# Attention's softmax in a fused attention and expert kernel: the maximum subtracted on VectorE, one exponential per half unit in a stage of its own

## The chip, the cores and the metric

One core of one Trainium2 chip runs the whole program. The metric is the device time of one execution in microseconds, as the median of several runs. The engines named below are TensorE (matrix products and transposes), VectorE, ScalarE, GpSimd and SyncE (whose queue, SP, issues nearly all transfers). Each engine takes its instructions in a fixed order, written at build time.

## What is computed

Three parts in a row, in fp32. First a chunked attention over 2 batches, 8 heads, 768 positions of 64 values, with 8 memory keys ahead of every chunk's own context. Then a layer of 4 experts, weighted by normalized probabilities. Then a two-matrix layer whose activation has a slope of its own for negative values.

```python
for c in range(nc):                       # chunks of 32; 16 keys to the left, 8 to the right
    scores = scale * np.matmul(q_c, k_full.transpose(0, 1, 3, 2))
    scores = scores - np.max(scores, axis=-1, keepdims=True)
    a = np.exp(scores)
    a = a / (np.sum(a, axis=-1, keepdims=True) + 1e-09)
    out[:, :, c_start:c_end] = np.matmul(a, v_full)
...
for e in range(E):
    h = np.maximum(x @ w1[e], 0.0)
    out += p[:, e:e + 1] * (h @ w2[e])
...
h = x @ w_in
g = np.maximum(h, 0.0) + alpha * np.minimum(h, 0.0)
return (g @ w_out).astype(np.float32)
```

## The kernel before

**Attention** is cut into 16 units of 96 queries (3 chunks, told apart by a mask that rides in extra rows of the operands) and each into two half units of 4 heads, 32 in all. `half_unit` (lines 191 to 246) is a generator; each `yield` ends a stage and gives the planner the lag until the next one. Its stages are these. (1) Four products `s` into one PSUM bank, 96x512; VectorE's maximum `mx` of each head; `nm`, the maximum times minus the scale, on VectorE; four exponentials on ScalarE, one per head, each with its `nm` as bias, from PSUM into `pe`. (2) Four transposes `t` of `pe` on TensorE, copied by ScalarE into `pt_ring`. (3) Four products `x` of `pt_ring` and the values, whose extra column of ones gives the denominator; `dn`, `rd` and the scaling into `xs_ring` on VectorE. (4) Two transposes `xt`, copied by ScalarE into `acc`; after a pair of units, `prep_x` makes the differences and the high and low parts of the next layer's input, on VectorE for the first two column blocks and on GpSimd for the others. `pe`, `pt_ring` and `xs_ring` have two slots each, by half unit; `qk` has three (`RING`) and `v` four (`RINGV`), and each is loaded again as soon as the stage that reads it has been written down.

**The planner.** There is no scheduler behind the kernel: `keep_in_program_order` holds each engine to the order in which the code calls it, and the code calls it along a planned clock `now`, which only TensorE's instructions move. `att_poll` (line 250) goes on with the first half unit whose lag is over, at most `LIVE` at a time, and starts a new one every `PACE`. Where nothing is due and it is forced, `fill` writes matmuls on a tile of zeros (`warm`) for the planned idle time. The lags are `LAT`, in planned us after each stage.

**Around it.** Names after the attention: `a`, `b`, `c`, `d` are the products of an expert's first matrix (`gemm1`, a fast scheme with seven products in place of eight), `y` those of the second (`gemm2`), each in a high and low split; `g` and `gg` are the activations, `wh` and `wl` the high and low part of the weights, made by a stream `prep_w` on ScalarE and VectorE (the first two pairs) or GpSimd. The columns go in two halves of 384. Attention is forced until 16 half units are done, enough for the first half; then come `gemm1` of the first pair for the first half (no attention in it, `hold`), `gemm2` with attention between its products, the forced rest of attention, and the same pair for the second half. From there on the work is expert products alone, with the conversion of the last layer's weights beside them.

Of the kernel before, what the change touches and what calls it, by code (L numbers as in the profile page):

```python
# [10 lines left out]
F32 = mybir.dt.float32  # L11
# [3 lines left out]
AF = mybir.ActivationFunctionType  # L15
ALU = mybir.AluOpType
# [4 lines left out]
BLK = 96  # L21
NCH = BLK // CH
KEYS = MEM + LEFT + BLK + RIGHT
DQ = D + NCH
NBLK = S // BLK
NU = B * NBLK
NT, DM = B * S, H * D
E, F1, F2 = 4, 1024, 2048
P = 128
# [33 lines left out]
def tile_kernel(ctx: ExitStack, tc: tile.TileContext, qk, mask, v, wa, wq, dpt, alpha, out):  # L63
    nc = tc.nc
    scale = 1.0 / float(D) ** 0.5
    pe_, dve, act, pool = (Pinned(tc, e) for e in (nc.tensor, nc.vector, nc.scalar, nc.gpsimd))

    cp = ctx.enter_context(tc.tile_pool(name="cp", bufs=1))
# [5 lines left out]
    def bank(name):  # L74
        return ps.tile([P, 512], F32, tag="ps", name=name)
# [14 lines left out]
    now = [0.0]  # L90

    def fill(n):

        if n > 0:
            wps = bank(f"wps{now[0]}")
            for _ in range(n):
                pe_.matmul(wps[:, :256], warm[:, :P], warm, start=True, stop=True)
                now[0] += 0.11
# [29 lines left out]
    def prep_x(c0, n, fast):  # L128
        cs = slice(c0, c0 + n)
        b11, b12 = acc[:, 0:2, 0, cs], acc[:, 0:2, 1, cs]  # L130
        b21, b22 = acc[:, 2:4, 0, cs], acc[:, 2:4, 1, cs]
        st = bp.tile([P, 4, 2, n], F32, tag="st", name=f"st{c0}")
        e = dve if fast else pool
        sub = ALU.subtract
        act.copy(xh[:, 0:4, cs], acc[:, :, 0, cs])
        e.tensor_tensor(out=st[:, 0], in0=b12, in1=b11, op=sub)
        yield
        e.tensor_tensor(out=st[:, 1], in0=b22, in1=st[:, 0], op=sub)
        act.copy(xh[:, 4:6, cs], b22)
        yield  # L140
        e.tensor_tensor(out=st[:, 2], in0=b22, in1=b12, op=sub)
        pool.tensor_tensor(out=xl[:, 0:4, cs], in0=acc[:, :, 0, cs], in1=xh[:, 0:4, cs].bitcast(F32), op=sub)
        yield
        e.tensor_tensor(out=st[:, 3], in0=b21, in1=st[:, 1], op=sub)
        pool.tensor_tensor(out=xl[:, 4:6, cs], in0=b22, in1=xh[:, 4:6, cs].bitcast(F32), op=sub)
        yield
        for z in (0, 2):
            r = slice(6 + 2 * z, 10 + 2 * z)
            t_ = st[:, z:z + 2].rearrange("p a b n -> p (a b) n")
            act.copy(xh[:, r, cs], t_)  # L150
            yield
            e.tensor_tensor(out=xl[:, r, cs], in0=t_, in1=xh[:, r, cs].bitcast(F32), op=sub)
            yield
# [6 lines left out]
    def mm(*a, n, passes=1, least=0.085, **kw):  # L160
        pe_.matmul(*a, **kw)
        now[0] += max(least, 0.011 + passes * n / 2.4e3)
# [10 lines left out]
    def load_half(hu):  # L173
        if hu >= 2 * NU:
            return
        u, half = divmod(hu, 2)
        tq = qk_t[hu % RING]
        kind = {0: 0, NBLK - 1: 2}.get(u % NBLK, 1)
        nc.sync.dma_start(tq[:D], qk[u, :, half])
        if kind_t[hu % RING] != kind:  # L180
            eng = nc.gpsimd if hu < RING else nc.sync
            eng.dma_start(tq[D:DQ], mask[kind])
            kind_t[hu % RING] = kind

    def load_v(hu):
        if hu >= 2 * NU:
            return
        u, half = divmod(hu, 2)
        nc.sync.dma_start(v_t[hu % RINGV // 2][:, hu % 2], v[u, :, half])

    def half_unit(u, half):

        hu = 2 * u + half
        tq, tv = qk_t[hu % RING], v_t[hu % RINGV // 2][:, hu % 2]
        tq = tq[:DQ]
        qv = tq[:, :QW].rearrange("p (h q) -> p h q", q=BLK)
        kv = tq[:, QW:].rearrange("p (h k) -> p h k", k=KEYS)
        vv = tv.rearrange("p (h d) -> p h d", d=D + 1)
        c, ab = divmod(u, 2)
        cols = slice(c * BLK, (c + 1) * BLK)  # L200
        hs = slice(2 * half, 2 * half + 2)
        nm = f"{u}_{half}"
        s_ps = bank(f"s{nm}").rearrange("p (h k) -> p h k", k=KEYS)
        for i in range(4):
            mm(s_ps[:BLK, i], qv[:, i], kv[:, i], n=KEYS, passes=4, start=True, stop=True)
        load_half(hu + RING)
        mx = cp.tile([P, 4], F32, tag="mx", bufs=4, name=f"mx{nm}")
        dve.tensor_reduce(out=mx[:BLK], in_=s_ps[:BLK], axis=AX.X, op=ALU.max)
        nm_ = cp.tile([P, 4], F32, tag="nm", bufs=4, name=f"nm{nm}")
        dve.tensor_scalar_mul(nm_[:BLK], mx[:BLK], -scale)  # L210
        pe = pe_t[hu % 2]
        for i in range(4):
            act.activation(
                pe[:BLK, i], s_ps[:BLK, i], AF.Exp, bias=nm_[:BLK, i:i + 1], scale=scale
            )
        yield LAT[0]
        t_ps = bank(f"t{nm}")[:, :4 * BLK].rearrange("p (h q) -> p h q", q=BLK)
        for i in range(4):
            pe_.transpose(t_ps[:, i], pe[:BLK, i], ident[:BLK, :BLK])
            now[0] += 0.085  # L220
        pt = pt_ring[:, hu % 2]
        act.copy(pt, t_ps)
        yield LAT[1]
        x_ps = bank(f"x{nm}")[:, :4 * (D + 1)].rearrange("p (h d) -> p h d", d=D + 1)
        for i in range(4):
            mm(x_ps[:BLK, i], pt[:, i], vv[:, i], n=D, passes=4, least=0.17, start=True, stop=True)
        load_v(hu + RINGV)
        dn = cp.tile([P, 4, 1], F32, tag="dn", bufs=2, name=f"dn{nm}")
        dve.tensor_scalar_add(dn[:BLK], x_ps[:BLK, :, D:D + 1], 1e-9)
        rd = cp.tile([P, 4, 1], F32, tag="rd", bufs=2, name=f"rd{nm}")  # L230
        dve.reciprocal(rd[:BLK], dn[:BLK])
        xs = xs_ring[:, hu % 2]
        dve.tensor_tensor(
            out=xs[:BLK], in0=x_ps[:BLK, :, :D], in1=rd[:BLK].to_broadcast([BLK, 4, D]),
            op=ALU.mult,
        )
        yield LAT[2]
        xt_ps = bank(f"xt{nm}")[:, :2 * BLK].rearrange("p (c q) -> p c q", q=BLK)
        xf = xs.rearrange("p h d -> p (h d)")
        for z in range(2):  # L240
            pe_.transpose(xt_ps[:, z], xf[:BLK, z * P:(z + 1) * P], ident[:BLK, :BLK])
            now[0] += 0.085
        act.copy(acc[:, hs, ab, cols], xt_ps)
        if ab == 1 and half == 1:
            for _ in prep_x(c * BLK, BLK, c < 2):
                yield 0.4

    att = {"next": 0, "start": 0.0, "done": 0, "over": set(), "live": []}

    def att_poll(force=False):  # L250

        while True:
            due = [x for x in att["live"] if x[0] <= now[0]]
            room = att["next"] < 2 * NU and len(att["live"]) < LIVE
            if due:
                x = due[0]
                try:
                    lat = next(x[1])
                    x[0] = now[0] + lat
                except StopIteration:  # L260
                    att["live"].remove(x)
                    att["over"].add(x[2])
                    while att["done"] in att["over"]:
                        att["done"] += 1
            elif room and att["start"] <= now[0]:
                g = half_unit(*divmod(att["next"], 2))
                att["start"] = now[0] + (PACE0 if force else PACE)
                att["next"] += 1
                x = [0.0, g, att["next"] - 1]
                att["live"].append(x)  # L270
                x[0] = next(g) + now[0]
            elif force:
                times = [x[0] for x in att["live"]]
                if room:
                    times.append(att["start"])
                t = min(times)
                fill(int((t - now[0]) / 0.11))
                now[0] = max(now[0], t)
                continue
            else:  # L280
                return
            if force:
                return
# [164 lines left out]
    def product(*a, n, **kw):  # L448
        if not hold[0]:
            att_poll()  # L450
        lag_poll()
        prep_poll()
        mm(*a, n=n, **kw)
# [204 lines left out]
USE = (A11, S2, S1, A12, S3, S4, A22)  # L658
SLOTS = 10

LAT = (2.6, 1.0, 1.4)
LIVE = 4
PACE = 2.3
PACE0 = 2.3
# [80 lines left out]
```

## Time and profile before

| | |
|---|---|
| median of 3 runs | 923.3 us (914.43 to 926.68) |
| profiled execution | 916.23 us, its span 914.5 us |
| TensorE busy | 870.7 us (95%) |
| VectorE busy | 622.9 us (68%) |
| ScalarE busy | 363.0 us (40%) |
| GpSimd busy | 571.2 us (62%) |
| granted TensorE clock, mean | 0.972 of full |

How to read it: the shares are averages over stages with different limits. Attention takes about the first 150 us, where TensorE waits and its clock falls; behind that TensorE is busy nearly all the time, but for a stretch about 600 to 700 us, between the two layers. What a change to attention is worth is read from the first 150 us.

### The profile page before, as it was taken

Reading aid. Unit: us, or ns where it says so; the run is one execution under the profiler, and the core shown is the slowest. Engines: PE = TensorE matmul, PEld = TensorE weight load, DVE = VectorE, ACT = ScalarE, POOL = GpSimd, SP = SyncE. Lnnn points to the kernel's source line nnn. Section 1 sums busy time; section 2 is a strip of 40 time slices with the busy share of each in tenths; the row PEclk is TensorE's granted clock in tenths of the full one; section 3 lists DMA queues with packets and bytes.
Section 4 is the critical chain, followed back from the end, with each engine's and each line's share of the span. In section 5 each row is a group of like instructions: output and inputs, shape, how many; then the busy total and the mean of one; then the engine's idle time right before and its main releaser. Section 6 shows DMA issues by size and latency. Waiting matters only on the chain.

```text
span 914.5 us, 14418 instructions
## 1 busy us (share of the span) xinstructions
PE 870.7 (95%) x5211; PEld 852.5 (93%) x5211; DVE 622.9 (68%) x1232; ACT 363.0 (40%) x874; POOL 571.2 (62%) x619
## 2 busy tenths in 40 slices
PE   8888779999999999999999999998689999999998
PEld 7778668999999999999999999997579999999998
DVE  4765444676777677767766676769987767765655
ACT  4655343222323232322232232324456556454632
POOL 1134333677768776777777787767559778775521
PEclk9789888999999999999999999999889999999999
DMA  7442220022223213321232223121102221211003
GB/s 187 127 146 70 65 78 24 24 70 92 79 72 104 72 56 100 120 70 59 81 105 73 89 81 104 47 82 42 61 15 101 93 80 37 87 53 47 1 1 138
DMA packets 29353, 69.36 MB, mean 76 GB/s; under 512 B 4536, under 2 KB 12856, under 8 KB 29282
## 3 DMA queue, kind: packets, MB, share of 16 engines
q1 hardware_dynamic: 29186, 68.41, 23.2%
q8 instruction: 41, 0.67, 0.3%
q14 instruction: 30, 0.25, 0.1%
q0 software_dynamic: 96, 0.03, 0.0%
HBM read 56.87 MB, written 11.56 MB: 75 GB/s over the span
## 4 chain that ended last, share of the span: by engine, by line
PE 86%; DVE 6%; ACT 4%; issue 1%; POOL 1%; DMA 1%; SPq 0%; ACTq 0%; DVEq 0%; POOLq 0%
PE y L57 42%; PE a L57 10%; PE d L57 10%; PE c L57 10%; PE b L57 5%; PE s L57 3%; PE x L57 3%; ACT pe L57 2%; DVE st L57 2%; DVE xl L57 1%; DVE mx L57 1%; PE t L57 1%; ACT pt_ring L57 1%; DVE g L57 1%; DMA qk<-in_mask 1%
## 5 line engine op out<-in xcount | busy, mean ns | idle before, releaser
L57 PE MATMUL y<-gg,wh 128*128 128x384 f32 x1540 | 404.8, 338 | 8.2 <-POOL gg L57 3.9
L57 PEld LDWEIGHTS y<-gg,wh 128*128 128x128 f32 x1540 | 280.7, 190 | 12.2 <-POOL gg L57 6.2
L57 POOL TENSOR_TENSOR gg<-g,gg 128x384 fp32r<-128x384 f32 x192 | 198.9, 1044 | 128.9 <-ACT gg L57 105.8
L57 PE MATMUL y<-gg,wl 128*128 128x384 f32 (+1 forms) x770 | 259.9, 337 | 0.0
L57 DVE TENSOR_TENSOR acc<-y,acc 128x384 f32<-128x384 f32 x353 | 188.5, 550 | 66.8 <-PE y L57 63.6
L57 ACT CAST gg<-g 128x384 fp32r<-128x384 f32 x192 | 97.6, 511 | 168.9 <-DVE g L57 168.7
L57 PEld LDWEIGHTS y<-gg,wl 128*128 128x128 f32 x770 | 146.2, 190 | 0.0
L57 POOL TENSOR_TENSOR wl<-raw,wh 128x256 fp32r<-128x256 f32 (+1 forms) x110 | 109.2, 1003 | 50.1 <-PE b L57 43.1
L57 ACT COPY u<-a 128x384 f32<-128x384 f32 x48 | 23.0, 479 | 215.9 <-PE a L57 215.7
L57 POOL TENSOR_TENSOR wl<-s,wh 128x256 fp32r<-128x256 f32 x88 | 67.7, 777 | 5.1 <-ACT wh L57 5.0
L57 PE MATMUL c<-xh,wh 128*128 128x384 f32 x192 | 64.9, 338 | 4.3 <-DVE b L57 4.3
L57 PE MATMUL d<-xh,wh 128*128 128x384 f32 x192 | 64.8, 337 | 0.6 <-DVE t L57 0.6
L57 PE MATMUL d<-xh,wl 128*128 128x384 f32 x192 | 64.6, 336 | 0.0
L57 PE MATMUL c<-xl,wh 128*128 128x384 f32 x192 | 64.6, 336 | 0.0
L57 PE MATMUL c<-xh,wl 128*128 128x384 f32 x192 | 64.6, 336 | 0.0
L57 PE MATMUL d<-xl,wh 128*128 128x384 f32 x192 | 64.6, 336 | 0.0
L57 PE MATMUL a<-xh,wh 128*128 128x384 f32 x192 | 64.5, 336 | 0.0
L57 PE MATMUL a<-xl,wh 128*128 128x384 f32 x192 | 64.4, 335 | 0.0
L57 DVE TENSOR_TENSOR u<-b,u 128x384 f32<-128x384 f32 x48 | 26.7, 556 | 55.2 <-PE b L57 51.2
L57 PE MATMUL a<-xh,wl 128*128 128x384 f32 x192 | 64.2, 334 | 0.0
L57 POOL TENSOR_TENSOR xl<-acc,xh 128x384 fp32r<-128x384 f32 (+1 forms) x32 | 27.6, 868 | 51.5 <-ACT xh L57 51.4
L57 ACT ACTIVATE pe<-s,nm 96x128 f32<-96x128 f32 x128 | 36.1, 360 | 58.0 <-DVE nm L57 41.5
(142 smaller groups left out, 1591.2 us busy)
## 6 DMA issues: line engine op xcount, KB each, us to landing
raw<-in_wa SPq DMA_DIRECT2D x32, 512.0 KB, 3.4
fr<-in_wq SPq DMA_DIRECT2D x32, 512.0 KB, 3.4
w2s<-fl SPq DMA_DIRECT2D x32, 256.0 KB, 2.8
raw<-w2s SPq DMA_DIRECT2D x16, 512.0 KB, 3.6
qk<-in_qk SPq DMA_DIRECT2D x32, 224.0 KB, 3.4
v<-in_v SPq DMA_DIRECT2D x32, 130.0 KB, 2.1
pb<-p_dram SPq DMA_DIRECT2D x8, 384.0 KB
outT<-acc SPq DMA_DIRECT2D x15, 192.0 KB, 2.0
```

The costliest lines, as they stand in the source:

```text
L57: return self.tc.keep_in_program_order(f(*a, **kw))
```

## The change

The product of the maximum and minus the scale goes. In its place VectorE subtracts the maximum from the scores, reading PSUM and writing 96x512 into `pe`; one exponential over 96x512 then runs on ScalarE, in place in `pe`, with the scale as its factor. It is a stage of its own, 1.5 planned us (`LATE`) after the first. The other lags become 1.2, 1.5 and 1.6 from 2.6, 1.0 and 1.4, so that the planned time of a half unit's stages goes from 5.0 to 5.8 us. `att_poll` counts each half unit's stages and holds one back (`clear`) where the half unit two before it has not gone far enough for the slot that it would use: it starts when that one has had its transposes `t`, writes `pt_ring` when that one has had `x`, and `xs_ring` when that one has had `xt`. Over the whole program `fill` writes 209 matmuls where it wrote 181.

```diff
--- before.py
+++ after.py
@@ -206,13 +206,13 @@
         load_half(hu + RING)
         mx = cp.tile([P, 4], F32, tag="mx", bufs=4, name=f"mx{nm}")
         dve.tensor_reduce(out=mx[:BLK], in_=s_ps[:BLK], axis=AX.X, op=ALU.max)
-        nm_ = cp.tile([P, 4], F32, tag="nm", bufs=4, name=f"nm{nm}")
-        dve.tensor_scalar_mul(nm_[:BLK], mx[:BLK], -scale)
         pe = pe_t[hu % 2]
-        for i in range(4):
-            act.activation(
-                pe[:BLK, i], s_ps[:BLK, i], AF.Exp, bias=nm_[:BLK, i:i + 1], scale=scale
-            )
+        dve.tensor_tensor(
+            out=pe[:BLK], in0=s_ps[:BLK], in1=mx[:BLK].unsqueeze(2).to_broadcast([BLK, 4, KEYS]),
+            op=ALU.subtract,
+        )
+        yield LATE
+        act.activation(pe[:BLK], pe[:BLK], AF.Exp, scale=scale)
         yield LAT[0]
         t_ps = bank(f"t{nm}")[:, :4 * BLK].rearrange("p (h q) -> p h q", q=BLK)
         for i in range(4):
@@ -245,16 +245,23 @@
             for _ in prep_x(c * BLK, BLK, c < 2):
                 yield 0.4
 
-    att = {"next": 0, "start": 0.0, "done": 0, "over": set(), "live": []}
+    att = {"next": 0, "start": 0.0, "done": 0, "over": set(), "live": [], "stage": [0] * 2 * NU}
+
+    NEED = {0: 3, 2: 4, 3: 5}
+
+    def clear(hu):
+        return hu < 2 or att["stage"][hu - 2] >= NEED.get(att["stage"][hu], 0)
+
 
     def att_poll(force=False):
 
         while True:
-            due = [x for x in att["live"] if x[0] <= now[0]]
-            room = att["next"] < 2 * NU and len(att["live"]) < LIVE
+            due = [x for x in att["live"] if x[0] <= now[0] and clear(x[2])]
+            room = att["next"] < 2 * NU and len(att["live"]) < LIVE and clear(att["next"])
             if due:
                 x = due[0]
                 try:
+                    att["stage"][x[2]] += 1
                     lat = next(x[1])
                     x[0] = now[0] + lat
                 except StopIteration:
@@ -269,8 +276,9 @@
                 x = [0.0, g, att["next"] - 1]
                 att["live"].append(x)
                 x[0] = next(g) + now[0]
+                att["stage"][x[2]] = 1
             elif force:
-                times = [x[0] for x in att["live"]]
+                times = [x[0] for x in att["live"] if clear(x[2])]
                 if room:
                     times.append(att["start"])
                 t = min(times)
@@ -658,7 +666,8 @@
 USE = (A11, S2, S1, A12, S3, S4, A22)
 SLOTS = 10
 
-LAT = (2.6, 1.0, 1.4)
+LAT = (1.2, 1.5, 1.6)
+LATE = 1.5
 LIVE = 4
 PACE = 2.3
 PACE0 = 2.3
```

How instructions now stand, at three places in the first half's `gemm2`, where attention runs between the `y`. In the names, `s11_0` is half 0 of unit 11; the number behind it is a buffer's. First ScalarE, before:

```order
L57 COPY pt_ring_109<-t11_0_1298 128x384
L57 COPY acc_103<-xt10_1_1305 128x2x96
L57 ACTIVATE pe0_110<-s12_0_1325,nm12_0_1333 96x128 x4
L57 COPY pt_ring_109<-t11_1_1339 128x384
L57 COPY acc_103<-xt11_0_1346 128x2x96
L57 ACTIVATE pe1_111<-s12_1_1366,nm12_1_1374 96x128 x4
```

and now (the exponential's half unit shows by its slot: `pe1` is s11_1, then `pe0` is s12_0, `pe1` s12_1):

```order
L57 COPY pt_ring_109<-t11_0_1214 128x384
L57 COPY acc_103<-xt10_1_1233 128x2x96
L57 ACTIVATE pe1_111<-pe1_111 96x512
L57 COPY pt_ring_109<-t11_1_1262 128x384
L57 COPY acc_103<-xt11_0_1268 128x2x96
L57 ACTIVATE pe0_110<-pe0_110 96x512
L57 COPY pt_ring_109<-t12_0_1298 128x384
L57 ACTIVATE pe1_111<-pe1_111 96x512
```

The copy of `t11_1` stood behind the exponentials of s12_0; now it stands ahead of them, right behind those of its own half unit.

TensorE over the same half units, before:

```order
L57 MATMUL x11_0_1314<-v1_108,pt_ring_109 96x65 x4
L57 MATMUL s12_0_1325<-qk0_104 96x128 x4
L57 MATMUL t11_1_1339<-ident_69,pe1_111 128x96 x4
L57 MATMUL y0_0_1_0_0_1183<-gg2_0_0_1138,wh2_0_657 128x384
L57 MATMUL xt11_0_1346<-ident_69,xs_ring_112 128x96 x2
L57 MATMUL y0_0_1_0_0_1183<-gg2_0_0_1138,wl2_0_658 128x384
L57 MATMUL y0_0_1_0_0_1183<-gg2_0_0_1138,wh2_0_657 128x384
L57 MATMUL y0_0_2_0_0_1214<-gg2_0_0_1138,wh2_0_657 128x384
L57 MATMUL y0_0_2_0_0_1214<-gg2_0_0_1138,wl2_0_658 128x384
L57 MATMUL x11_1_1355<-v1_108,pt_ring_109 96x65 x4
L57 MATMUL s12_1_1366<-qk1_105 96x128 x4
```

and now:

```order
L57 MATMUL x11_0_1237<-v1_108,pt_ring_109 96x65 x4
L57 MATMUL y0_0_1_0_0_1103<-gg2_0_0_1063,wh2_0_551 128x384
L57 MATMUL s12_0_1250<-qk0_104 96x128 x4
L57 MATMUL y0_0_1_0_0_1103<-gg2_0_0_1063,wl2_0_552 128x384
L57 MATMUL y0_0_1_0_0_1103<-gg2_0_0_1063,wh2_0_551 128x384
L57 MATMUL t11_1_1262<-ident_69,pe1_111 128x96 x4
L57 MATMUL xt11_0_1268<-ident_69,xs_ring_112 128x96 x2
L57 MATMUL y0_0_2_0_0_1132<-gg2_0_0_1063,wh2_0_551 128x384
L57 MATMUL y0_0_2_0_0_1132<-gg2_0_0_1063,wl2_0_552 128x384
L57 MATMUL y0_0_2_0_0_1132<-gg2_0_0_1063,wh2_0_551 128x384
L57 MATMUL y0_0_3_0_0_1149<-gg2_0_0_1063,wh2_0_551 128x384
L57 MATMUL s12_1_1278<-qk1_105 96x128 x4
```

The product `x11_1` stood ahead of the scores s12_1 and now stands behind them; one more `y` lies between `x11_0` and the scores s12_0, and two between those and `t11_1`.

VectorE, before:

```order
L57 TENSOR_SCALAR nm11_1_1292<-mx11_1_1290 96x4
L57 COPY acc_103<-y0_0_0_0_0_1140 128x384
L57 TENSOR_SCALAR dn11_0_1320<-x11_0_1314 96x4
L57 RECIPROCAL rd11_0_1322<-dn11_0_1320 96x4
L57 TENSOR_TENSOR xs_ring_112<-x11_0_1314,rd11_0_1322 96x256
L57 TENSOR_REDUCE mx12_0_1331<-s12_0_1325 96x4
L57 TENSOR_SCALAR nm12_0_1333<-mx12_0_1331 96x4
```

and now:

```order
L57 TENSOR_TENSOR pe1_111<-s11_1_1220,mx11_1_1226 96x512
L57 COPY acc_103<-y0_0_0_0_0_1065 128x384
L57 TENSOR_SCALAR dn11_0_1243<-x11_0_1237 96x4
L57 RECIPROCAL rd11_0_1245<-dn11_0_1243 96x4
L57 TENSOR_TENSOR xs_ring_112<-x11_0_1237,rd11_0_1245 96x256
L57 TENSOR_REDUCE mx12_0_1256<-s12_0_1250 96x4
L57 TENSOR_TENSOR pe0_110<-s12_0_1250,mx12_0_1256 96x512
L57 COPY acc_103<-y0_0_1_0_0_1103 128x384
L57 COPY acc_103<-y0_0_2_0_0_1132 128x384
```

The subtraction stands where the small product `nm` stood, and two evacuations of `y` follow where one did.

## Rows read from the trace of the kernel before

**Rows 1.** busy us (count) of five engines by stretch; clock, DMA share, GB/s
```profile
4.87:76.76 71.89, 61.27 (x524) 56.78 (x524) 45.11 (x132) 42.88 (x140) 14.44 (x19) 0.88 0.54 146
76.76:150.18 73.42, 60.96 (x438) 55.02 (x436) 30.15 (x85) 31.10 (x100) 24.95 (x34) 0.86 0.21 58
150.18:914.50 764.32, 744.66 (x4239) 737.93 (x4236) 547.46 (x1014) 287.58 (x632) 529.46 (x559) 0.99 0.21 71
```

**Rows 2.** waits of TensorE, 0 to 77 and 77 to 150; of VectorE, 77 to 150
```profile
...
PE x L57 <- ACT pt_ring L57: 10.0, 8, 1.9
...
PE x L57 <- ACT pt_ring L57: 10.4, 9, 1.9
...
DVE dn L57 <- PE x L57: 28.4, 12, 3.4
...
```

**Rows 3.** the chain that ended last, 112.25 to 116.89: start, us, what
```profile
112.25 0.89 PE x L57 x8
113.15 0.92 PE s L57 x8
114.09 0.70 DVE mx L57
...
115.34 1.13 ACT pe L57 x4
116.47 0.37 ACT pt_ring L57
116.89 0.89 PE x L57 x8
```

**Rows 4.** timeline of TensorE: start, us, what, waited before; three of its rows
```profile
25.54 1.09 PE L57 MATMUL x<-v,pt_ring 128*96 128x65 f32 x8 [1.84 <-ACT pt_ring L57]
...
84.63 1.04 PE L57 MATMUL s<-qk 67*96 67x128 f32 x8
...
136.00 1.96 PE L57 MATMUL s<-qk 67*96 67x128 f32 x8
```

**Rows 5.** busy time by stretches, as rows 1: two stretches at a low clock
```profile
26.00:36.00 10.00, 10.00 (x57) 9.38 (x56) 6.53 (x22) 4.38 (x16) 0.33 (x1) 0.50 0.29 76
134.00:147.00 13.00, 11.87 (x71) 10.42 (x72) 2.93 (x11) 4.44 (x15) 2.92 (x4) 0.61 0.08 32
```

**Rows 6.** groups by shape, 0 to 160: busy us, mean ns, idle before
```profile
L57 DVE TENSOR_REDUCE mx<-s 96x4 f32<-96x512 f32 x32 | 21.9, 685 | 17.9 <-PE s L57 17.2
...
L57 DVE TENSOR_SCALAR nm<-mx 96x4 f32<-96x4 f32 x32 | 5.9, 185 | 1.8
...
L57 DVE TENSOR_TENSOR xs_ring<-x,rd 96x256 f32<-96x256 f32 x32 | 13.5, 421 | 1.1
...
L57 DVE COPY acc<-y 128x384 f32<-128x384 f32 x8 | 4.2, 549 | 3.3 <-PE y L57 3.2
...
L57 DVE TENSOR_TENSOR wl<-raw,wh 128x512 fp32r<-128x512 f32 x3 | 2.5, 826 | 1.1 <-ACT wh L57 1.0
...
L57 ACT ACTIVATE pe<-s,nm 96x128 f32<-96x128 f32 x128 | 36.1, 360 | 58.0 <-DVE nm L57 41.5 <-DVE dn L57 4.7 <-PE y L57 4.7
...
L57 ACT COPY pt_ring<-t 128x384 f32<-128x384 f32 x32 | 15.5, 484 | 3.9 <-PE t L57 3.8
...
L57 ACT COPY acc<-xt 128x192 f32<-128x192 f32 x32 | 10.4, 325 | 7.1 <-PE xt L57 7.1
```

**Rows 7.** the chain, three pieces of TensorE at full clock, and attention's tail
```profile
20.45 0.34 PE t L57 x4
...
76.30 0.65 PE x L57 x8
...
78.06 1.04 PE b L57 x6
...
147.84 0.33 ACT acc L57
...
152.52 1.15 PE b L57 x5
```

## The prediction

> **What bounds the kernel now.** I read the busy time by stretches first, with three cuts: stretch A from the first scores to the first expert product, B from there to the second half's first product, and the rest [rows 1]. Attention has all its 32 half units in A (scores of 20) and B (scores of 12); A takes 71.89 us, B 73.42, the rest 764.32. In the rest TensorE is busy for 744.66 of 764.32 us at a granted clock of 0.99, and nothing there is edited, so the sum is made on A and B alone: 145.3 us, of which TensorE waits for 71.89 - 61.27 = 10.6 and 73.42 - 60.96 = 12.5.
>
> Next the list of waits for TensorE in both stretches: 10.0 and 10.4 us of these are the product `x` waiting for ScalarE's copy `pt_ring` [rows 2]. The chain says why [rows 3]. Read it as a loop: `x` (0.89), the scores behind it (0.92), VectorE's maximum (0.70), `nm`, the four exponentials (1.13), the copy `pt_ring` (0.37), and `x` again: 112.25 to 116.89, 4.64 us per half unit. The copy belongs to half unit h, but ScalarE has the exponentials of h+1 in front of it, and these need scores that stand on TensorE behind the preceding `x`. So each half unit waits for the next one's softmax. From s10_0 (84.63) to s15_1 (136.00) these loops make 51.4 us for 11 half units, 4.67 each [rows 4].
>
> The clock is second: granted 0.88 in A and 0.86 in B [rows 1], so at most 0.12 x 71.89 + 0.14 x 73.42 = 18.9 us go to it. It is 0.50 in 26 to 36 and 0.61 in 134 to 147 [rows 5].
>
> **The change, part by part.**
>
> *VectorE.* `nm` goes (185 ns each), a subtraction over 96x512 from PSUM comes. The trace has none. Nearest rows with a PSUM operand: 96x256 in 421 ns and 128x384 in 549, 1.0 ns per column, so 0.68 for 512; the maximum reads the same 512 columns in 685 [rows 6]. Lower end 0.55 (the 384-column row), upper 0.83 (the 512-column `wl`, also rows 6). I take 0.68. That adds 0.50 per half unit: 20 x 0.50 = 9.9 us in A, 5.9 in B. VectorE's busy time becomes 45.1 + 9.9 = 55.0 in A and 30.2 + 5.9 = 36.1 in B.
>
> *ScalarE.* Four exponentials (1.13 us in rows 3, 0.36 each alone) become one of 96x512. Copies of 192 and 384 columns take 325 and 484 ns, 0.83 per column, so 0.59 for 512 [rows 6]; the upper end is that nothing is saved, 1.13. I take 0.60. ScalarE frees 0.5 us per half unit; it is busy for 42.9 of 71.9, so the freed time as such is worth nothing. Path from scores to weights: 0.69 + 0.19 + 1.13 = 2.01 before, 0.69 + 0.68 + 0.60 = 1.97 after. The softmax is no shorter either.
>
> *The order.* This is what pays. With the exponential a stage of its own, ScalarE in B now has the copy right behind its own exponential or behind one whose scores are long done (order blocks of ScalarE and TensorE). I walked the changed order by hand with row durations at full clock [rows 3, 6, 7]: scores 0.90, `x` 0.65, `y` 0.17 each (a product's six matmuls take 1.04), `t` 0.34, copies and evacuations as their groups say, denominator, reciprocal and scaling together 0.75 (0.42 the scaling, the small ones near the 0.185 of `nm`), every start at the later of its operand and its engine's release. One turn, from the start of `x11_0` at 0: `x` ends at 0.65, one `y` at 0.82, scores s12_0 at 1.72, two `y` at 2.06. `t11_1` needs the exponential of s11_1. Those scores ended at -0.7; maximum and subtraction end at 0.7, the exponential at about 1.4, so no wait: `t11_1` ends at 2.40 and its copy at 2.93. `xt11_0` needs the scaling on VectorE, which follows an evacuation of 0.55 and ends at 2.0: no wait, 2.57. Four `y` to 3.25, s12_1 to 4.15, then `x11_1`, whose copy is 1.2 us old. The copy that held `x` nine times for 10.4 us in all is early.
>
> What is late next is VectorE: maximum 0.69, subtraction 0.68, three small ones 0.75 and, from s11_1 on, eight evacuations of 0.55 over six half units, 0.73: 2.85 us per half unit against some 2.6 of TensorE (scores 0.90, `x` 0.65, `t` 0.34, `xt` 0.17, three `y` 0.52). The walk gives 33.1 us for the 11 half units where rows 4 have 51.4, 3.0 each. Ahead of s10_0 B keeps its product of 7.9 us (84.63 - 76.76), plus 0.5 because `xt8_1`, `x9_0` and `t9_1` now stand before the scores. Behind s15_1 it goes from 14.2 us (150.18 - 136.00) to 10.6: the last half unit alone, then GpSimd's differences, 4.7 us from 147.84 to 152.52, which no edit touches and which hold the second half's product `b` [rows 7]. B: 8.4 + 33.1 + 10.6 = 52 us.
>
> A is walked the same way. Here VectorE also makes the first weights' low parts, and it is behind TensorE nearly throughout. The walk ends A, the product `a`, at 69 in place of 76.76; half of A gains nothing, and the rest comes when the weights' low parts get fewer. Of these 64 us VectorE is busy for 55.0, its 45.1 of before and the 9.9 added, and idle for 9 where it now is for 71.9 - 45.1 = 26.8: 1.4 ahead of the first maximum, the rest at the scalings, which wait for `x`, and at weight parts, which wait for ScalarE. At the bounds: 55 us with no idle time, and 72 or more if its idle time hardly shrinks.
>
> *More filler.* The planner issues 209 filler matmuls where it issued 181: 28 x 0.11 = 3.1 us of TensorE, inside the walk, covered where VectorE is behind. Without that cover (the tail) they cost their 0.11 each. Slots of `pe`, `xs_ring` and `pt_ring` stay two deep; loads of `qk` and `v` are issued at the same stage of their half unit, so SP's queue keeps its order, and A's 146 GB/s [rows 1] become 146 x 72/64 = 164. Work behind `hold` and the weight streams moves with the planner's clock and stays in place.
>
> *The clock.* The walk is at full clock. Where waits go, part of the 18.9 us should come back; VectorE's idle covers some of the rest. But 26 to 36 shows 0.50 with TensorE busy for 10.00 of 10.00 us [rows 5], behind a wait of 1.84 [rows 4]: a wait's cost runs on after it. A keeps waits of the old kind, since TensorE there waits for VectorE, and the tail of B its fillers. I put 3 us on A and 4 on B. The Trainium skill, TensorE: Matmul & The Clock Gate, Part 1, says that the slow state is the default and activity releases it; by that alone the 18.9 us would all come back and the 7 us here would be nothing, and the row at 0.50 while busy agrees only in part.
>
> **Sum.** 64 + 3 + 52 + 4 = 123 for A and B, against 145.3: 22 us less. The profiled execution took 916.2 us (span 914.5), which gives 894; the median of the runs is 923.3, 0.8% higher. I say 897.
>
> **Rivals.**
> 1. *VectorE binds harder.* Subtraction at 0.83 with an idle gap behind each wait: 0.15 x 32 = 4.8 us, and 7 more if A gains nothing (A has VectorE at 77% by the walk's start and 86% in it). Gain 22 - 12 = 10: 907. For it: the first half of A in the walk. Against: VectorE waits 28.4 us for `x` in B alone [rows 2], room that the 5.9 us fit in. The Trainium skill, Perfetto Trace Analysis, Optimizing Scalar/DVE Operations, advises moving work from a saturated VectorE to ScalarE; this change moves it the other way, and rows 1 agree that VectorE, at 63% of A, is the fuller (ScalarE 60%).
> 2. *The clock stays where it is.* Waits go, but the granted clock stays at 0.87: 18.9 in place of 7 us, gain 10, 906. For it: 0.61 in the tail among fillers. Against: 0.99 in the last 764 us [rows 1], where the work is dense.
> 3. *Slower: the exponential comes too late.* On ScalarE it now stands behind copies of `xt`, which need VectorE's scaling, which stands behind another's subtraction. If that loop (`x` 0.65, scaling 0.75 behind a maximum 0.69 and a subtraction 0.68, `xt` 0.33, copy 0.33, exponential 0.60, `t` 0.34, copy 0.48: 4.85) turned once per half unit and not once per two, A's 20 would take 97 us, 25 more, and B's 11 53.4, 2 more: 943. It decides from (71.9 + 51.4)/31 = 4.0 us per half unit. Against it: in the walk two half units share each turn, which takes 6 to 7 us.
> 4. *It does not do what it says:* the copy still behind a late exponential in most half units; then the time is that of before, 916 to 923. The order blocks speak against it in B, and for it in two places in A, where a pair of exponentials stands ahead of a copy.
>
> **Chances.** Forecast 0.60 (885 to 904); first rival 0.16, second 0.13, third 0.06, fourth 0.05. The low end is the whole walk at full clock, 916.2 - 29 = 887, less the lower subtraction; the high end takes in the first two rivals on the median's base, 907 x 923.3/916.2 = 914. Faster by over 2% (about what a measurement here can tell from no change) needs 18.5 us: nearly all of the forecast, 0.57, and 0.04 of the first two rivals at their better end: 0.61. Slower is the third rival, 0.06; within 2% is what is left, 0.33.
>
> **What would show it.** Right: `x` waiting for `pt_ring` under 5 us in all; scores in B every 3 us; the subtraction at 0.68 and the exponential at 0.6; `a` at 67 to 72 and the second half's `a` near 128; the rest still 764 us. Wrong: half units of 4 us in B with waits for `pe` or `xs_ring` (VectorE late), a clock under 0.9 in B, or a rest that is longer than 764.

## The result, and the profile after

The changed kernel takes 892.29 us (median of 4 runs, 892.18 to 895.23) beside 924.99 for the kernel before (4 runs, 914.43 to 927.32): a ratio of 0.968, 95% interval 0.960 to 0.975. Its profiled execution took 892.18 us, its span 890.4, at a mean granted clock of 0.978.

Busy time by the same three stretches as [rows 1], in the changed kernel (length, then busy us and count of TensorE, its weight loads, VectorE, ScalarE and GpSimd, then granted clock, DMA share, GB/s):

```profile
4.87:72.93 68.06, 61.77 (x528) 56.95 (x528) 51.74 (x130) 33.93 (x83) 13.93 (x19) 0.87 0.57 152
72.93:126.21 53.28, 52.19 (x461) 49.78 (x459) 35.62 (x87) 26.36 (x62) 25.24 (x34) 1.00 0.30 82
126.21:890.40 764.19, 746.86 (x4239) 740.77 (x4236) 546.00 (x1014) 287.53 (x632) 530.49 (x559) 0.99 0.21 71
```

A went from 71.89 to 68.06, B from 73.42 to 53.28, the rest from 764.32 to 764.19. Of the 24.1 us, 20.1 come from B and 3.8 from A. (One half unit's `x`, scaling and `xt` now lie behind A's end, 144 matmuls of `x` where there were 152, so about 0.8 us of A's gain is TensorE's work that has moved into B.) In B TensorE waits for 53.28 - 52.19 = 1.1 us where it waited for 12.5, and its clock is 1.00 where it was 0.86. In A the clock stands where it stood, and VectorE is busy for 76% of the stretch where it was for 63%.

The waits of TensorE in A and, below the gap, in B (us in total, times, longest), against [rows 2]:

```profile
PE xt L57 <- DVE xs_ring L57: 5.8, 6, 2.0
PE t L57 <- ACT pe L57: 0.4, 1, 0.4
...
PE s L57 <- ACT pt_ring L57: 0.6, 1, 0.6
PE x L57 <- ACT acc L57: 0.4, 1, 0.4
```

The 20.4 us in which `x` waited for `pt_ring` are gone from both lists. What is left in A is `xt` waiting for VectorE's scaling.

The chain that ended last in A, in two pieces, where [rows 3], taken from B, showed a loop over three engines (start, us, what):

```profile
13.48 0.61 DVE mx L57
...
14.18 0.69 DVE pe L57
14.87 0.33 DVE s L57
15.20 0.08 DVE dn L57
15.31 0.18 DVE rd L57
15.52 0.43 DVE xs_ring L57
...
53.60 1.71 PE s L57 x8
55.31 0.32 PE xt L57 x2
```

In the first piece the chain stays on VectorE, from one instruction to the next: a maximum, a subtraction, a sum of weights (`s`), and the scaling of another half unit. It does so for most of 11 to 32 us and of 40 to 51. In between, and from 52 us to A's end, it lies mostly on TensorE, and in the second piece the scores take 1.71 us, where [rows 3] have 0.92. Added up, A's chain has 29.0 us of VectorE and 34.9 of TensorE. So VectorE bounds about the first half of A, and TensorE, in part at a low clock, the second.

The new instructions, as groups by shape over 0 to 140 us, against [rows 6] (busy us, mean ns, idle before):

```profile
L57 DVE TENSOR_TENSOR pe<-s,mx 96x512 f32<-96x512 f32 x32 | 22.0, 687 | 2.8 <-DVE mx L57 0.5
...
L57 ACT ACTIVATE pe<-pe 96x512 f32<-96x512 f32 x32 | 20.2, 630 | 14.4 <-DVE pe L57 14.4
```

The subtraction takes 687 ns, the exponential 630, where four of them took 1.13 us in a row [rows 3].

Five rows of TensorE's timeline, as [rows 4]:

```profile
32.00 0.39 PE L57 MATMUL xt<-ident,xs_ring 96*128 96x96 f32 x2 [1.97 <-DVE xs_ring L57]
...
33.67 1.91 PE L57 MATMUL s<-qk 67*96 67x128 f32 x8
...
81.47 1.04 PE L57 MATMUL s<-qk 67*96 67x128 f32 x8
...
116.19 1.04 PE L57 MATMUL s<-qk 67*96 67x128 f32 x8
...
128.55 0.44 PE L57 MATMUL b<-xl,wh 128*128 128x384 f32 x1 [0.75 <-POOL xl L57]
```

From s10_0 (81.47) to s15_1 (116.19) B's 11 half units take 34.72 us, 3.16 each, where they took 51.4. In A a wait of 1.97 us for VectorE at 32.00 is followed by scores that take 1.91 us in place of 1.04.

Three stretches of the changed kernel (columns as above):

```profile
30.00:40.00 10.00, 8.03 (x46) 7.73 (x46) 5.78 (x19) 2.45 (x6) 0.00 (x0) 0.62 0.62 164
50.00:60.00 10.00, 8.57 (x58) 8.04 (x58) 6.92 (x19) 4.79 (x12) 4.47 (x7) 0.66 0.37 99
...
81.47:116.19 34.72, 33.63 (x307) 32.09 (x306) 26.91 (x67) 19.45 (x45) 16.11 (x23) 1.00 0.41 114
```

A loses its clock mostly in two pieces, 0.62 and 0.66; [rows 5] showed such pieces before. In B's loop TensorE is busy for 33.63 of 34.72 us: it is TensorE itself that bounds there now.

### The profile page after: what moved, and what is told of

Same layout as the page of the kernel before. It is cut to its first block, busy times and chain, and to the rows that moved or that the text cites. A ratio compares the mean times of both kernels' runs of the same rounds, so it can differ in the third digit from the quotient of the medians.

```text
span 890.4 us, 14374 instructions
## 1 busy us (share of the span) xinstructions
PE 864.6 (97%) x5239; PEld 850.3 (95%) x5239; DVE 633.5 (71%) x1232; ACT 349.3 (39%) x778; POOL 572.1 (64%) x619
## 4 chain that ended last, share of the span: by engine, by line
PE 88%; DVE 9%; issue 1%; ACT 1%; POOL 1%; DVEq 0%; POOLq 0%; ACTq 0%
PE y L57 43%; PE a L57 11%; PE d L57 11%; PE c L57 11%; PE b L57 5%; PE s L57 2%; DVE st L57 2%; PE x L57 2%; DVE xl L57 1%; PE t L57 1%; DVE pe L57 1%; DVE mx L57 1%; DVE g L57 1%; DVE acc L57 1%; PE xt L57 1%
## 5 line engine op out<-in xcount | busy, mean ns | idle before, releaser
L57 DVE TENSOR_TENSOR u<-b,u 128x384 f32<-128x384 f32 x48 | 26.7, 557 | 55.6 <-PE b L57 51.4
L57 ACT CAST wh<-raw 128x256 fp32r<-128x256 f32 (+1 forms) x120 | 55.7, 488 | 0.6 <-PE a L57 0.6
```

What stands on the lines that cost most here:

```text
L57: return self.tc.keep_in_program_order(f(*a, **kw))
```

## The experiments

The change has three parts: other operations (the subtraction, one exponential), a stage boundary ahead of the exponential, and longer lags behind it. My theory was that the stage boundary breaks the loop, that the operations are worth nothing by themselves, and that the lags matter little. The rivals were that any longer lag does as much, and that the operations are what pays. Each time below is a median beside that of the kernel before, run beside it on the same chip, and the ratio is to that; A and B are those of one profiled execution.

**The operations alone.** Subtraction and single exponential, both still in the first stage, with the old lags and the old planner.

```diff
-        nm_ = cp.tile([P, 4], F32, tag="nm", bufs=4, name=f"nm{nm}")
-        dve.tensor_scalar_mul(nm_[:BLK], mx[:BLK], -scale)
...
-        for i in range(4):
-            act.activation(
-                pe[:BLK, i], s_ps[:BLK, i], AF.Exp, bias=nm_[:BLK, i:i + 1], scale=scale
-            )
+        dve.tensor_tensor(
+            out=pe[:BLK], in0=s_ps[:BLK], in1=mx[:BLK].unsqueeze(2).to_broadcast([BLK, 4, KEYS]),
+            op=ALU.subtract,
+        )
+        act.activation(pe[:BLK], pe[:BLK], AF.Exp, scale=scale)
```

> The operations alone: maximum, subtraction and one exponential of 96x512 in the first stage, as before's four exponentials stood there; the lags and the planner of before. Theory (the order pays, the operations don't): the copy pt_ring still stands behind the next half unit's exponential, the path from scores to weights is 0.69 + 0.69 + 0.63 = 2.01 us as before's 2.01, and VectorE has 0.5 us more per half unit; so TensorE's wait for pt_ring stays at some 20 us and the time at that of before, 910 to 925. Rival (ScalarE's shorter exponential pays): the changed kernel's 892 nearly or quite.

Measured: 913.54 us beside 922.53, ratio 0.993 (0.989 to 0.997). A 69.92, B 74.44. The chain of this kernel in B, one turn (start, us, what):

```profile
107.08 0.89 PE x L57 x8
107.97 0.92 PE s L57 x8
...
108.91 0.70 DVE mx L57
...
109.70 0.70 DVE pe L57
...
110.42 0.63 ACT pe L57
111.05 0.37 ACT pt_ring L57
...
111.47 0.89 PE x L57 x8
```

It is the loop of [rows 3] with `nm` and four exponentials replaced by a subtraction and one exponential: 4.39 us a turn where it was 4.64. The copy still stands behind the next half unit's exponential, and `x` still waits for `pt_ring`, for 9.2 us in A and 6.9 in B (20 expected in all). The operations alone give under 1%.

**The order alone.** `nm` and the four exponentials as before, but the exponentials as a stage of their own, with the change's lags and its `clear`.

```diff
         dve.tensor_scalar_mul(nm_[:BLK], mx[:BLK], -scale)
         pe = pe_t[hu % 2]
+        yield LATE
         for i in range(4):
...
-LAT = (2.6, 1.0, 1.4)
+LAT = (1.2, 1.5, 1.6)
+LATE = 1.5
```

> The order alone: nm and the four exponentials of before, but the exponentials in a stage of their own (LATE 1.5), with the changed kernel's lags and its clear. Theory (the order pays): wait for pt_ring nearly gone, A and B as in the changed kernel or shorter, since VectorE is rid of 0.5 us per half unit where it is behind in A; 885 to 897. Rival (the shorter exponential on ScalarE is needed too): ScalarE's 1.13 us makes the copies late again, 905 or more.

Measured: 893.05 us, ratio 0.971 (0.965 to 0.978), as much as the whole change. A and B of this kernel (columns as above):

```profile
4.72:70.34 65.62, 61.98 (x529) 55.34 (x528) 43.83 (x131) 42.16 (x140) 13.59 (x19) 0.92 0.59 159
70.34:124.58 54.24, 52.81 (x461) 50.21 (x459) 31.63 (x86) 32.19 (x101) 25.29 (x34) 1.00 0.30 81
```

B is that of the changed kernel within 1 us, though ScalarE is busy for 6 us more. The order is what pays.

**Longer lags without the stage.** Operations and stages as before; the first lag 2.7 (1.5 and 1.2 together), the others 1.5 and 1.6, with `clear` counted for the stages that there are.

```diff
+    NEED = {0: 2, 1: 3, 2: 4}
...
-LAT = (2.6, 1.0, 1.4)
+LAT = (2.7, 1.5, 1.6)
```

> The longer lags alone: nm and four exponentials in the first stage as before, lags 2.7, 1.5 and 1.6 (5.8 in all as in the changed kernel), with clear fitted to three stages. Theory (the exponential's own place on ScalarE pays): a new half unit starts 2.3 planned us after the last one and brings its exponentials ahead of the copy at 2.7, so pt_ring stays late and the time is 905 to 925. Rival (any longer lag would do): 890 to 900.

Measured: 895.05 us, ratio 0.973 (0.967 to 0.980); A 68.38, B 57.92. **My theory fell here**, and the rival held: no stage boundary is needed. The timelines of TensorE and, below the last gap, of ScalarE show why:

```profile
99.41 1.11 PE L57 MATMUL s<-qk 67*96 67x128 f32 x8
100.55 0.89 PE L57 MATMUL x<-v,pt_ring 128*96 128x65 f32 x8
101.28 0.50 PE L57 MATMUL t<-ident,pe 96*128 96x96 f32 x4
...
106.75 0.89 PE L57 MATMUL x<-v,pt_ring 128*96 128x65 f32 x8 [0.75 <-ACT pt_ring L57]
...
99.01 1.13 ACT L57 ACTIVATE pe<-s,nm 96x128 f32<-96x128 f32 x4 [2.19 <-DVE nm L57]
100.03 0.48 ACT L57 COPY pt_ring<-t 128x384 f32<-128x384 f32 x1
```

The copy still stands behind the next half unit's exponentials, but the next scores now stand ahead of `x` on TensorE, so these exponentials no longer wait for that `x`. The loop has two edges, places where one instruction stands behind another: the copy behind the exponentials on ScalarE, and the next scores behind `x` on TensorE. The stage opens the first, the longer lags open the second, and either brings most of the gain. Some of the wait is left: `x` waits for `pt_ring` for 5.9 us in A and 3.0 in B, and B is 4 us longer than with the stage.

**One lag alone.** As that, but with only the lag ahead of `x` longer (`clear` with the old lags gives the old order row for row, so what acts here is the lag).

```diff
-LAT = (2.7, 1.5, 1.6)
+LAT = (2.6, 1.5, 1.4)
```

> The kernel before with one lag changed, transposes to x 1.5 in place of 1.0 (lags 2.6, 1.5, 1.4; clear for three stages, which by itself leaves the order as it was). The scores s12_1 now stand ahead of x11_1 on TensorE, while the copies still stand behind the next half unit's exponentials on ScalarE. New theory (the loop has two edges, copy behind exponentials on ScalarE and scores behind x on TensorE, and dies when either goes): 893 to 902, with pt_ring still waited for some 9 us. Rival (all three longer lags together matter, or the time planned for them): 905 to 920.

Measured: 906.05 us beside 917.33, ratio 0.987 (0.982 to 0.992); A 68.74, B 67.08 at a clock of 0.85. The waits of TensorE in its B:

```profile
PE t L57 <- DVE xs_ring L57: 2.6, 2, 1.6
PE x L57 <- ACT pe L57: 2.0, 1, 2.0
PE x L57 <- ACT pt_ring L57: 1.6, 4, 0.7
```

The wait for the copy is 1.6 us in place of 10.4, but half of that has gone to two other waits, and the clock has not come back: B gains 6 us, not 20. I expected more than this; the rival's range held it. So the theory that the loop dies when either edge goes is not borne out by this lag: about half of the wait that it removes comes back elsewhere.

**The stage alone, in both forms.** First the change with the old lags behind the exponential, then the same with `nm` and four exponentials, thus the order-alone kernel with those lags.

```diff
-LAT = (1.2, 1.5, 1.6)
+LAT = (1.2, 1.0, 1.4)
```

> The changed kernel with the lags behind the exponential short as before (1.2, 1.0, 1.4): the exponential keeps its own stage and its copy stands ahead of the next exponential, but x11_0 stands right behind t11_0 and ahead of the scores again. Theory of the two edges: 890 to 900, waits for pt_ring under 6 us. Rival (only the lag ahead of x matters, the own stage does nothing): 905 to 920.

> The stage alone: nm and the four exponentials of before, the exponentials 1.5 planned us later in a stage of their own, all other lags as short as before's (1.2, 1.0, 1.4 behind it; clear for four stages). Theory (the place of the exponential on ScalarE is enough): A 65 us, B 52 to 54, 885 to 892. Rival (stage, longer lags and shorter exponential are needed together): 900 or more.

Measured: 887.19 us beside 917.33 for the first, ratio 0.968 (0.963 to 0.972); 882.35 (880.43 to 883.10) beside 916.86 for the second, ratio 0.960 (0.954 to 0.965). A and B of the second:

```profile
4.88:65.32 60.44, 56.74 (x544) 52.20 (x543) 43.06 (x131) 41.75 (x139) 15.24 (x20) 1.00 0.70 172
65.32:117.42 52.10, 50.72 (x448) 48.56 (x446) 32.34 (x86) 32.87 (x101) 24.31 (x33) 1.00 0.31 84
```

Both times are under what my theory said (890 to 900, and 885 to 892). The stage boundary suffices by itself; behind it the longer lags are not needed. (From the scores to the transposes 1.5 + 1.2 = 2.7 planned us go by, where 2.6 did before.) Without the subtraction VectorE is busy for 43.06 us of A, and A runs at full clock. B is the same in both forms (51.84 and 52.10).

Since the changed kernel had run on another chip than this version, it was run again.

> The changed kernel itself once more, in more rounds, because the runs of it and of the kernel with the stage of its own and short lags alone (882.35 us) stand on different chips. If that version is really the better one, this gives 889 to 895 us, a ratio of 0.963 to 0.973 to the kernel before, with a first stretch of 65 to 69 us and its granted clock under 0.95. If the chip made the difference, it gives 885 or less and a first stretch near 62 us.

Measured: 892.71 us (890.94 to 894.29) beside 918.35, ratio 0.972 (0.968 to 0.975); A 67.20 at 0.87, B 53.26 at 1.00. The stage alone is about 10 us faster than the change. The chips are still two, but each ratio is to the kernel before on its own chip, and their intervals don't meet.

**The subtraction done twice.** The change with its subtraction written twice; the second one writes the same values over the first's.

```diff
+        dve.tensor_tensor(
+            out=pe[:BLK], in0=s_ps[:BLK], in1=mx[:BLK].unsqueeze(2).to_broadcast([BLK, 4, KEYS]),
+            op=ALU.subtract,
+        )
```

> The changed kernel with the subtraction done twice (the same values written again), 0.69 us more of VectorE per half unit. Theory (VectorE is what A is bound by now, and B has room): A longer by 8 to 14 of the 13.7 us added to its 20 half units, B by 2 to 5 of 8.2; 902 to 911 in all. Rival (VectorE is hidden in both): at most 3 us more, 892 to 895.

Measured: 908.12 us beside 922.53, ratio 0.986 (0.983 to 0.990). A, B and a piece of A:

```profile
4.88:90.31 85.43, 76.26 (x528) 70.42 (x528) 64.39 (x149) 34.47 (x83) 14.25 (x19) 0.70 0.46 122
90.31:150.03 59.72, 55.19 (x462) 51.33 (x459) 44.08 (x100) 26.49 (x62) 24.89 (x34) 0.97 0.27 73
...
60.00:80.00 20.00, 20.00 (x111) 18.92 (x110) 11.82 (x27) 8.27 (x20) 6.77 (x9) 0.50 0.22 64
```

The added 20 x 0.687 = 13.7 us of VectorE make A 17.4 us longer in this execution, and A's clock falls from 0.87 to 0.70. In B 12 x 0.687 = 8.2 us make 6.4. Both are above what I expected (8 to 14, and 2 to 5), though the median is inside 902 to 911. That VectorE is not hidden in A is shown. Most of the lengthening comes by the clock: TensorE waits for 9.17 us where it waited for 6.29, and is shown busy for 76.26 where it was for 61.77; from 60 to 80 it is busy throughout, at 0.50, and VectorE for 11.82 us only. (The profiled execution is the longest of this kernel's ten, 5.7 us above their median, so A's 17.4 is at its upper end. By the medians, run apart, all 22.0 us added cost 15.8, 908.12 against 892.29.)

**VectorE's load lowered.** The differences of the second column block move from VectorE to GpSimd: first on the order-alone kernel, then on the change, then on both with the short lags.

```diff
-            for _ in prep_x(c * BLK, BLK, c < 2):
+            for _ in prep_x(c * BLK, BLK, c < 1):
```

> The order alone (nm and four exponentials in a stage of their own), and the input differences of the second column block moved from VectorE to GpSimd: four differences and two low parts, 8 operations or some 3.5 us of VectorE in A, onto an engine that is busy for 13.9 of 68.1 us there. Theory (VectorE binds A): A shorter than with the order alone by 2 to 4 us, 888 to 892. Rival (TensorE's clock and order bind A): same as the order alone, 893.

> The changed kernel with the same move of the second column block's differences from VectorE to GpSimd. Theory (VectorE binds A): A shorter by 2 to 4 us, 888 to 890. Rival: no change, 892.

> The changed kernel with the short lags (1.2, 1.0, 1.4) and the second column block's differences on GpSimd: the two edits that each gave A or B a little. Theory (they add): A 64, B 52, 883 to 887. Rival (they do not add): as the short lags alone, 887.

> The stage alone with the second column block's differences on GpSimd, so that VectorE has least to do in A. Theory (VectorE and the clock that follows its waits bind A): A 62, B 52 to 54, 882 to 888, the best of all. Rival (ScalarE, with 42 us of work in A, binds first): 889 or more.

Measured, beside 917.33: 891.82 us for order alone (886.48 to 899.10; ratio 0.975, 0.968 to 0.981) and 889.49 for the change (887.77 to 892.03; ratio 0.970, 0.965 to 0.974). Beside 916.86: 885.46 for the change with short lags (884.74 to 886.33; ratio 0.964, 0.958 to 0.969) and 883.52 for the stage alone (883.28 to 884.64; ratio 0.962, 0.955 to 0.968). A of the four, in this order:

```profile
4.88:66.88 62.00, 58.36 (x528) 51.56 (x528) 41.87 (x125) 42.26 (x140) 19.02 (x25) 1.00 0.65 167
```

```profile
4.88:69.33 64.45, 59.47 (x528) 54.75 (x528) 49.30 (x124) 34.06 (x83) 18.84 (x25) 0.92 0.61 161
```

```profile
4.88:69.52 64.64, 58.28 (x544) 52.99 (x543) 49.75 (x123) 33.67 (x82) 19.25 (x25) 0.97 0.61 160
```

```profile
4.50:66.29 61.79, 56.90 (x543) 51.92 (x543) 42.37 (x125) 41.76 (x139) 20.32 (x26) 1.00 0.71 169
```

Each of the first three has an A about 3 us shorter than the same kernel without the move (65.62, 68.06, 67.41), at a higher clock. The move is six operations, and VectorE's busy time in A fell by 2.0, 2.4 and 1.4 us there, less than the 3.5 expected. The medians show about that for the change (889.49 against 892.7), less for the others, and none of it stands clear of the intervals; the first's profiled execution is its fastest, 5.3 us under its median. On the stage alone the move gains nothing (883.52 against 882.35, run beside each other): A already ran at full clock with VectorE idle for 17 us, and I had expected it to be the best of all. The last two, run beside each other too, differ in the operations alone: the subtraction and the single exponential cost 1.9 us there, with ranges that don't meet.

## Why the prediction was right, point by point

**The loop.** Right. That the copy stands behind the next half unit's exponentials, and these behind `x`, was read from [rows 3]; the waits of 20.4 us were forecast to fall under 5 and fell to none of that pair. It was too narrow as an account of why: the loop has a second edge, on TensorE, and the longer lags alone, by opening that one, do nearly as much (895.05 us), though one of them alone does not (906.05). The order blocks ahead of the prediction showed both edges move, and I spoke of the first.

**The operations.** Their prices were right, 0.68 for 0.687 and 0.60 for 0.630, and so was it that they don't pay: 1% without the new order, nothing with it and the long lags (893.05 and 892.71), a loss of 1.9 to 4.8 us with the short ones (885.46 and 883.52; 887.19 and 882.35, on two chips).

**B.** 56 was forecast, 53.28 measured. The walk's pieces: 8.4 ahead of s10_0 (81.47 - 72.93 = 8.54), 33.1 for the 11 half units (34.72), 10.6 behind s15_1 (126.21 - 116.19 = 10.02). The 4 us for the clock were the failed term: it was 1.00 throughout, tail included, though the tail has its fillers as before. What the walk got wrong inside is who is late next: it named VectorE at 2.85 us per half unit against TensorE's 2.6. Measured over the 11 half units are 26.91 / 11 = 2.45 for VectorE and 33.63 / 11 = 3.06 for TensorE, which hardly waits. The 2.6 counted three `y` per half unit, where all 48 `y` lie in these 11, and no filler, of which 14 do.

**A.** 67 forecast, 68.06 measured, out of parts that were wrong both ways, so that the total comes so near is luck. (`a` starts at 72.93, just outside the 67 to 72 named as a sign.) VectorE is busy for 51.74 us, not 55.0: the subtractions cost their 20 x 0.687 = 13.7 and `nm`'s 3.2 went, but the other instructions on it took 51.74 - 13.7 = 38.0 where they had taken 45.11 - 3.2 = 41.9. The clock's term was 3 us; at 0.87 it may be up to 0.13 x 68.06 = 8.8. The runs with more and less work on VectorE bear out that its lateness has a part in this: 0.70 at 64.39 us busy, 0.87 at 51.74, 0.92 at 49.30, 1.00 at 43.06. It is not all, since the order alone has 0.92 at 43.83 and the operations alone 0.95 at 54.23. The lags behind the exponential matter as well: at nearly the same work on VectorE the short ones have a higher clock than the long ones, 0.92 (51.12 us busy) against 0.87 (51.74), and 1.00 (43.06) against 0.92 (43.83). With the short lags A also holds more fillers, 129 matmuls against 114 or 115, and no run tells the two apart.

**The clock and the skill.** In the prediction the Trainium skill, TensorE: Matmul & The Clock Gate, Part 1, stood for the case that all of the clock comes back. In B the trace agrees (1.00). In A that case did not come true (0.87); TensorE goes on waiting there, for 6.3 us, so A does not speak against the page.

**The rivals.** The first, that VectorE binds harder, was priced at 907. It does bind in the first half of A, as the chain shows, and the doubled subtraction shows that it is not hidden, but with enough idle time left that A still gains 3.8 us. The advice cited there, the Trainium skill, Perfetto Trace Analysis, Optimizing Scalar/DVE Operations, agrees with the runs in part: giving the work back to ScalarE is worth about 7 us of A and 1.9 to 5 us of the median with short lags, nothing with long ones. The second rival, the clock that stays, held in A and failed in B. The third, an exponential too late at 4.85 us a turn, did not come: `t` waits for `pe` for 0.4 us in A and not at all in B. The fourth did not come either.

**The base.** To the sum of 894 I added 3 us, since the median of before was 0.8% above its profiled execution (0.8% would have been 7). The changed kernel's profiled execution stands on its median (892.18 and 892.29), so the sum itself was nearer. What the change gives against the medians is thus 32.7 us on paper and 25.6 beside the larger set of runs (892.71 beside 918.35), which is about the 24.1 that the stretches show.

**What stays open.** Why the long lags behind the stage cost 10 us with the old operations (893.05 and 882.35) is settled in part: 5 us of it lie in A, 2 in B, 3 in the rest. In A TensorE waits equally long (3.64 and 3.70 us) but is busy for 61.98 us at 0.92 against 56.74 at 1.00, so these 5 us are the clock's. In B the long lags have 81 fillers where the short ones have 64, at 0.11 us each 1.9 of the 2.1. Why the clock of A falls with the long lags, and whether the 3 us of the rest (764.62 and 761.28) come from them, stays open. So does why VectorE's other instructions in A took 3.9 us less in the changed kernel; some 0.75 of that is the scaling, with `dn` and `rd`, that moved into B (17 of each in A where there were 18).

## What to carry to other kernels

Where an engine waits again and again for a short copy, look at what stands ahead of that copy on its own engine, and follow the chain until it comes back to the instruction that waited: such a loop can be opened at more than one of its edges, and a stage boundary at the long operation does it without making anything cheaper. Opening an edge may leave new waits behind, as the single longer lag did (906.05). Try that boundary alone, with the old lags and the old operations, before rewriting the operations or stretching the other lags: here the stage alone was 4.0% under the kernel before, and nothing that was added to it gained any. Work added to an engine that is already late can cost TensorE its clock too, so read the clock's column before and after: with the subtraction done twice, that was most of what A lost in the profiled execution.

## What the runs showed of the hardware

That a piece can stand at 0.50, the lower of the two levels (1.2 of 2.4 GHz), for 20 us in which TensorE is shown busy for 20.00 was not expected at that length: with the doubled subtraction, as in [rows 5] for 10 us, a low clock goes on in a stretch that shows no waiting. The busy share does not show it there, and the clock's column does. Nor does the sum of the waits in a stretch tell its clock. In B the clock went from 0.86 to 1.00 as TensorE's waits went from 12.5 to 1.1 us, and in A 9.2 us of waits stand with 0.70 (doubled subtraction) and 6.3 with 0.87 (the change). But the kernel with the operations alone waits for 12.75 us in A at 0.95 and for 8.4 in B at 0.79:

```profile
4.66:74.58 69.92, 57.17 (x526) 52.03 (x524) 54.23 (x132) 33.62 (x83) 14.73 (x19) 0.95 0.56 151
74.58:149.02 74.44, 66.04 (x438) 59.11 (x436) 36.38 (x85) 24.55 (x61) 24.96 (x34) 0.79 0.20 57
```

In all nine profiles whose B holds 1.5 us of waits or less, the clock of B is 1.00; where more are left, what a stretch loses was not to be read from their sum.
